# Batch 0's last kv from two terms, a later output copy, and two loads exchanged, in a fused attention and feed-forward kernel

## Chip, core, metric

One core of one Trainium2 chip. The time is that of one execution on the device in microseconds (us). Each kernel is run several times and checked against the reference; all runs told here were correct and none was more than 1.5% above the fastest run of its kernel. Profiles come from one further execution, and their times count from the start of the span.

## The reference, cut to what matters

```python
def phi(x): return where(x > 0, x, exp(x) - 1) + 1     # = max(x, 0) + min(exp(x), 1)
q_p, k_p = phi(q), phi(k)                              # (8 batches, 8 heads, 576, 64)
kv  = einsum('bhsd,bhse->bhde', k_p, v)
z   = sum(k_p, axis=2)
x   = (q_p . kv) / (q_p . z + 1e-6)                    # -> (4608 tokens, 512)
out = (silu(x @ w_gate) * (x @ w_val)) @ w_out         # d_ff = 1536
```

## The kernel before, cut

Tokens go through the feed-forward part in nine groups of 512. Almost all of the time is matmuls of 128x128 by 128x512. What is not hidden is the head: batch 0's attention has to be done before the first feed-forward matmul. The head pairs of a batch are `lp` 0 and 1; "x" is a normalised attention output, the operand of the first layer.

```python
r_copy(0, 0, 1, "VV")             # kv of pair 0 -> R (VectorE)
add_k(0, 1)                       # phi(k) of pair 1: min(exp k,1) + max(k,0)
t_corners(0, R, 0, X)             # numerators of pair 0
x_t(0, 0, X)                      # two x of pair 0 (VectorE)
kv_corner(0, 1, kp, True, True)   # kv of pair 1: 36 matmuls of 64x64
r_copy(0, 1, 2, "VV")
warm(WARM[7], ps=pp4[2][1])       # one matmul that only fills
l1_mm(0, 0, pp4[2], (0,))         # first feed-forward matmuls (L276)
l1_mm(0, 1, X, (0,))
t_corners(0, R, 1, pp4[1])
x_t(0, 1, pp4[1])
... (l1_mm for chunks 1, 2, 3; then the other blocks, L292)
```

Weights and the next batches' k, q and v are loaded by GpSimd on one queue (q0 of the page). They land in the order in which it issues them: of the loads below, those issued at 22.25, 23.57, 24.97 and 26.65 us in the kernel before land at 34.1, 35.5, 38.0 and 39.4. Group 0's second layer (L299) is interleaved with batch 1's attention: transposes of phi(q) (L370), then its x, then group 1's first matmuls.

```python
ld_w2(0, 4); ld(q, qr, 1, 0); ld_w2(4, 8); ld(q, qr, 1, 1); ld_w2(8, 12)
...
for t in range(4):
    if t == 3: nx(0, dz); nx(1, cq)             # numerators and x of batch 1
    for fb in range(FO, FB): l2_mm(0, t, fb)
    if t < 3: l2_out(0, t, "V")                 # output copy on VectorE
exp_k(2, 0); exp_k(2, 1)
l2_out(0, 3, "V")
```

## Time and profile before

| | before |
|---|---|
| time, median of 3 runs | 314.3 us (314.2 to 314.55) |
| span of the profile | 312.5 us |
| TensorE busy | 306.2 us, 98% |
| first feed-forward matmul (L276) starts | 14.34 us |
| batch 1's transposes (L370) start | 40.77 us |
| group 1's first matmul (L276) starts | 49.84 us |

In the profile PE is TensorE's matmuls, PEld its weight loads, DVE VectorE, ACT ScalarE, POOL GpSimd. A line of a timeline is: start, time, engine, line of the source, operation, out<-in, shapes, count, and in brackets the idle time before it and what ended it. Matmuls overlap: one of 512 columns shows 0.38 us, but in this trace the next starts 0.215 to 0.216 us after it. Below, a wait of TensorE is the distance of two starts less 0.2155.

### The profile page before, as it was taken

How to read it: one execution, taken by the hardware profiler on the slowest of the kernel's cores; microseconds unless marked ns; L12 is line 12 of the kernel's file. 1: busy time of each engine (PE TensorE's matmuls, PEld its weight loads, DVE VectorE, ACT ScalarE, POOL GpSimd, SP SyncE). 2: the span in 40 equal slices, each digit the busy share in tenths (PEclk: the TensorE clock that was granted, in tenths of full speed). 3: DMA queues.
4: the chain of work that ended last, by engine and by line, in shares of the span. 5: the costliest groups of instructions: out<-in, count | busy, mean ns of one | idle time of the engine just before them, and what ended most of it. 6: DMA issues, size and time to landing. Idle time of an engine off the chain costs nothing.

```text
span 312.5 us, 5494 instructions
## 1 busy us (share of the span) xinstructions
PE 306.2 (98%) x2169; PEld 142.3 (46%) x2169; DVE 204.0 (65%) x361; ACT 153.9 (49%) x232; POOL 47.4 (15%) x72
## 2 busy tenths in 40 slices
PE   8999999999999999999999999999999999999994
PEld 3444454444544454445444544454444444444442
DVE  4854859899699657976697759874981434143410
ACT  4955869639733845375535643475330333133311
POOL 8655334310000410032000500000000000000000
PEclk9999999999999999999999999999999999999999
DMA  8999999997512594139612990324032300140014
GB/s 218 198 196 200 207 206 240 231 206 127 116 26 41 92 192 117 38 50 183 171 37 39 131 235 3 73 45 92 2 69 57 86 1 1 39 97 0 0 36 101
DMA packets 41162, 32.80 MB, mean 105 GB/s; under 512 B 16432, under 2 KB 36144, under 8 KB 41136
## 3 DMA queue, kind: packets, MB, share of 16 engines
q0 software_dynamic: 20464, 18.29, 37.4%
q1 hardware_dynamic: 20592, 14.13, 18.8%
q8 instruction: 17, 0.28, 0.4%
q14 instruction: 9, 0.07, 0.1%
q10 hardware_dynamic: 80, 0.03, 0.0%
HBM read 37.75 MB, written 9.44 MB: 151 GB/s over the span
## 4 chain that ended last, share of the span: by engine, by line
PE 95%; DMA 1%; DVE 1%; ACT 1%; issue 0%; SPq 0%; DVEq 0%
PE pp L292 57%; PE pp L299 30%; PE pp L276 2%; PE pp L254 2%; PE pp L185 2%; DMA q<-in_q_dram 1%; PE pp L124 0%; ACT ek L120 0%; PE pp L398 0%; PE pp L370 0%; PE pp L429 0%; DVE xT L411 0%; ACT qT L120 0%; DVE kp L159 0%; PE pp L212 0%
## 5 line engine op out<-in xcount | busy, mean ns | idle before, releaser
L120 ACT ACTIVATE sil<-pp 128x512 f16<-128x512 f32 x108 | 63.4, 597 | 101.8 <-PE pp L292 100.0
L292 PE MATMUL pp<-xT,wg 128*128 128x512 f16 x416 | 106.8, 379 | 0.0
L292 PE MATMUL pp<-xT,wv 128*128 128x512 f16 x416 | 106.8, 379 | 0.0
L285 DVE SCALAR_TENSOR_TENSOR hT<-pp,sil 128x512 f16<-128x512 f32 x108 | 72.4, 681 | 48.8 <-PE pp L292 35.5
L299 PE MATMUL pp<-wo,hT 128*128 128x512 f16 (+2 forms) x444 | 97.1, 373 | 0.6 <-DVE osb L322 0.6
L299 PEld LDWEIGHTS <-hT 128*128 128x128 f16 x444 | 42.0, 98 | 49.8 <-issue 2.1
L292 PEld LDWEIGHTS <-wv 128*128 128x128 f16 x416 | 40.7, 98 | 49.1
L292 PEld LDWEIGHTS <-wg 128*128 128x128 f16 x416 | 40.7, 98 | 48.4
L322 DVE TENSOR_SCALAR osb<-pp 128x512 f32<-128x512 f32 (+1 forms) x19 | 12.9, 682 | 30.9 <-PE pp L299 26.5
L120 ACT ACTIVATE osb<-pp 128x512 f32<-128x512 f32 (+1 forms) x18 | 10.3, 574 | 34.8 <-PE pp L299 34.8
L120 ACT ACTIVATE ek<-kr 128x1152 f16<-128x1152 f16 x16 | 17.9, 1157 | 0.1
L120 ACT ACT_TABLE_LOAD x13 | 16.7, 1283 | 2.3 <-PE pp L292 2.1
L229 DVE TENSOR_TENSOR qp<-qp,rden 128x1152 f16<-128x1152 f16 x12 | 16.2, 1347 | 0.0
L220 DVE TENSOR_REDUCE den<-prod 128x18 f32<-128x1152 f16 x12 | 16.1, 1343 | 0.0
L120 ACT ACTIVATE eq<-qr 128x1152 f16<-128x1152 f16 (+1 forms) x15 | 16.0, 1102 | 0.1
L695 POOL COPY gate<-qT 128x1 f16<-128x1 f16 x4 | 1.0, 256 | 97.2 <-DMA qT<-qp 97.2
L271 DVE TENSOR_SCALAR xT<-pp 128x512 f16<-128x512 f32 (+1 forms) x14 | 8.8, 667 | 7.1 <-PE pp L254 7.1
L103 POOL DMA_DIRECT2D vr<-in_v_dram x16 | 11.7, 731 | 8.5 <-PE pp L292 2.6
L103 POOL DMA_DIRECT2D kr<-in_k_dram x16 | 11.5, 723 | 8.9 <-DMA vr<-in_v_dram 2.8
L159 DVE TENSOR_TENSOR kp<-ek,kp 128x1152 f16<-128x1152 f16 x16 | 12.1, 758 | 0.5
L103 POOL DMA_DIRECT2D qr<-in_q_dram x14 | 10.3, 736 | 6.7 <-DMA wo<-in_moe_w_out_dram 1.7
L147 DVE TENSOR_SCALAR ek<-ek 128x1152 f16<-128x1152 f16 x16 | 7.5, 470 | 5.7 <-ACT ek L120 5.5
(82 smaller groups left out, 179.5 us busy)
## 6 DMA issues: line engine op xcount, KB each, us to landing
out_dram<-osb SPq DMA_DIRECT2D x70, 128.0 KB, 3.4
kr<-in_k_dram POOLq DMA_DIRECT2D x16, 288.0 KB, 8.6
vr<-in_v_dram POOLq DMA_DIRECT2D x16, 288.0 KB, 9.9
qr<-in_q_dram POOLq DMA_DIRECT2D x14, 288.0 KB, 11.9
wo<-in_moe_w_out_dram POOLq DMA_DIRECT2D x3, 512.0 KB, 13.0
wg<-in_moe_w_gate_dram POOLq DMA_DIRECT2D x5, 256.0 KB, 8.7
wv<-in_moe_w_val_dram POOLq DMA_DIRECT2D x5, 256.0 KB, 9.3
q<-in_q_dram SPq DMA_DIRECT2D x2, 576.0 KB, 4.1
```

Of the source, the lines that this page charges most:

```text
L103: nc.gpsimd.dma_start(out=dst[b % NB][:, 2 * lp:2 * lp + 2, :], in_=src[b].rearrange("(l a) (c j) d -> (a c) l (j d)", a=2, j=J)[:, 2 * lp ...
L120: nc.scalar.activation(out=out, in_=in_, func=func, bias=bias, scale=scale)
L147: nc.vector.tensor_scalar(out=a, in0=a, scalar1=1.0, scalar2=None, op0=ALU.min)
L159: nc.vector.tensor_tensor(out=a, in0=ek[b % 2][:, lp, :, :], in1=a, op=ALU.add)
L185: nc.tensor.matmul(out=ps[hh][D * l2:D * l2 + D, D * lp:D * lp + D], lhsT=t[b % 2][rows, lp, j, D * l2:D * l2 + D], rhs=vr[b % NB][rows, 2 ...
L220: nc.vector.tensor_reduce(out=den[:, c, :], in_=prod[:, :, :].rearrange("p j (l d) -> p (j l) d", d=D), axis=AX.X, op=ALU.add)
L229: nc.vector.tensor_tensor(out=qv, in0=qv, in1=rden[:, c, :].unsqueeze(2).to_broadcast([P, 2 * J, D]), op=ALU.mult)
L271: nc.vector.tensor_scalar(out=dst, in0=ps[l2][:, c0:], scalar1=1.0 / SC, scalar2=None, op0=ALU.mult)
L285: nc.vector.scalar_tensor_tensor(out=hT[g % 2][:, fb, :], in0=ps[1][:, :], scalar=SC, in1=s[:, :], op0=ALU.mult, op1=ALU.mult)
L292: nc.tensor.matmul(out=ps[h][:, :], lhsT=w[:, c, P * fb:P * fb + P], rhs=xT[g % 2][:, c, :], start=(c == 0), stop=(c == 3))
L299: nc.tensor.matmul(out=l2p[(g, t)][:, n0:n1], lhsT=hT[g % 2][:, fb, P * t:P * t + P], rhs=wo[:, fb, n0:n1], start=(fb == 0), stop=(fb == F ...
L322: nc.vector.tensor_scalar(out=o[:, n0:n1], in0=ps[:, n0:n1], scalar1=1.0 / SC, scalar2=None, op0=ALU.mult)
```

## The change

The intent is to take waits out of the head and one from ahead of group 1. VectorE no longer makes phi(k) of pair 1; TensorE sums kv over both terms of it instead. The copies of R go between the first two x. Group 0's third output copy makes way for batch 1's x. And w_out's second third is loaded ahead of q, so that it is there in time for a second layer that starts earlier.

```diff
-    WARM = (4, 1, 4, 3, 2, 1, 1, 1)
+    WARM = (4, 1, 4, 3, 2, 1, 1)
@@ loads
     ld_w2(0, 4)
+    ld_w2(4, 8)
     ld(q, qr, 1, 0)
-    ld_w2(4, 8)
     ld(q, qr, 1, 1)
@@ head
-    add_k(0, 1)
     t_corners(0, R, 0, X)
-    x_t(0, 0, X)
-    kv_corner(0, 1, kp, True, True)
+    x_t(0, 0, X, (0,))
+    kv_corner(0, 1, kp, True, False)
+    kv_corner(0, 1, ek, False, True)
     r_copy(0, 1, 2, "VV")
-    warm(WARM[7], ps=pp4[2][1])
+    x_t(0, 0, X, (1,))
     l1_mm(0, 0, pp4[2], (0,))
+    t_corners(0, R, 1, pp4[1])
     l1_mm(0, 1, X, (0,))
-    t_corners(0, R, 1, pp4[1])
@@ group 0's second layer
-            if t < 3:
+            if t < 2:
                 l2_out(0, t, "V")
         exp_k(2, 0)
         exp_k(2, 1)
+        l2_out(0, 2, "V")
         l2_out(0, 3, "V")
```

## The prediction

What no trace or run of this case shows is cut out of the recorded text, and with it one of its four rivals. No term of its sum is among the cuts: it still comes to -0.10 + 0.18 - 0.20 = -0.12 us.

> **What bounds the kernel now.** I read the page first (busy shares), then the chain of work that ended last, then TensorE's waits, then the timelines of VectorE, TensorE and GpSimd around the three places that the change touches, and last the landings of single transfers. All times are microseconds from the start of the span.
>
> From the page:
>
> ```profile
> PE 306.2 (98%) x2169; PEld 142.3 (46%) x2169; DVE 204.0 (65%) x361; ACT 153.9 (49%) x232; POOL 47.4 (15%) x72
> ```
>
> TensorE is busy 98% of 312.5 us, and the chain puts 95% of the span on it. So a change can move the end only where TensorE waits, or where its own work grows or shrinks. After 52 us it hardly waits: a feed-forward stage in the chain is 96 matmuls in 20.72 us, 215.8 ns each. The listed waits are all at the head, except one of 0.6 us at the very end, which the change leaves alone. What the change can win is therefore in the first 50 us. The chain there:
>
> ```profile
> 12.98 0.68 DVE kp L159
> ...
> 13.70 0.48 PE pp L185 x36
> 14.18 0.32 PE pp L124
> 14.50 0.86 PE pp L276 x4
> ...
> 49.11 0.69 DVE xT L411
> ```
>
> The reader is to see that the chain crosses VectorE at 12.98 (the add that makes phi(k) for the second head pair) and at 49.11 (the first x of group 1). Between them it goes through the filler matmul L124 into the first L276 matmuls. The change attacks both crossings. VectorE's timeline at the first:
>
> ```profile
> 12.90 0.75 DVE L159 TENSOR_TENSOR kp<-ek,kp 128x1152 f16<-128x1152 f16 x1
> 13.56 1.28 DVE L411 SCALAR_TENSOR_TENSOR xT<-pp,rd 128x512 f16<-128x512 f32 x2
> 14.76 0.35 DVE L201 CAST R<-pp 128x64 f16<-128x64 f32 x2
> 15.81 1.29 DVE L411 SCALAR_TENSOR_TENSOR xT<-pp,rd 128x512 f16<-128x512 f32 x2 [0.70 <-PE pp L254]
> ```
>
> The kv result (R) was ready at 14.2, but its copies stand behind two x and start at 14.76. At the second crossing, in VectorE's and TensorE's timeline:
>
> ```profile
> 48.50 0.69 DVE L322 TENSOR_SCALAR osb<-pp 128x512 f32<-128x512 f32 x1 [0.18 <-PE pp L299]
> ...
> 49.11 2.47 DVE L411 SCALAR_TENSOR_TENSOR xT<-pp,rd 128x512 f16<-128x512 f32 x4
> ...
> 49.84 0.38 PE L276 MATMUL pp<-xT,wg 128*128 128x512 f16 x1
> ```
>
> The third output copy of group 0 stands directly ahead of the x that TensorE waits for. TensorE's last matmul before it starts at 49.41 (three from 48.96, about 0.22 apart), so it could go on at 49.62 and goes on at 49.84: 0.22 lost.
>
> The third place is in between. TensorE transposes batch 1's phi(q), which VectorE makes from a q that has to land:
>
> ```profile
> 37.63 0.29 DVE L392 TENSOR_TENSOR qp<-eq,qr 128x256 f16<-128x256 f16 x1
> 37.84 0.45 DVE L374 TENSOR_SCALAR qp<-qr 128x1152 f16<-128x1152 f16 x1
> 38.29 0.46 DVE L147 TENSOR_SCALAR ek<-ek 128x1152 f16<-128x1152 f16 x1
> ...
> 39.95 0.76 DVE L377 TENSOR_TENSOR qp<-qp,eq 128x1152 f16<-128x1152 f16 x1
> ```
>
> ```profile
> 40.77 0.62 PE L370 MATMUL pp<-id,qp 128*128 128x128 f16 x8
> ```
>
> The add ends at 40.71, the transposes start at 40.77. TensorE's last matmul before started at 40.51 and would have let it go on at 40.72. VectorE is just in time; nothing here is spare. GpSimd's timeline of issues and, for the two issues, the landings:
>
> ```profile
> 23.57 0.70 POOL L103 DMA_DIRECT2D qr<-in_q_dram  x1 [0.56 <-DMA wv<-in_moe_w_val_dram]
> 24.97 0.76 POOL L116 DMA_DIRECT2D wo<-in_moe_w_out_dram  x1 [0.71 <-DMA kr<-in_k_dram]
> ```
>
> ```profile
> qr<-in_q_dram POOLq DMA_DIRECT2D x1, 288.0 KB, 11.9
> ```
>
> ```profile
> wo<-in_moe_w_out_dram POOLq DMA_DIRECT2D x1, 512.0 KB, 13.0
> ```
>
> The last number is microseconds from issue to landing: q lands at 23.57 + 11.9 = 35.5, w_out's second third at 24.97 + 13.0 = 38.0. The same view gives the first third at 34.1 and q's second half at 39.4.
>
> [...]
> - [...] The page's PEclk row is 9 in all slices[...].
> - [...] from the L276 matmul at 14.98 to the 64x64 corners at 15.29 are 0.31 us, not 0.22; about 0.09 per switch.
> - [...] The landings above come in the order of issue, so exchanging two issues exchanges who lands first.
> - [...] 0.70 us spans, 11.9 us landings. So I use landings only.
>
> **The change part by part.**
>
> *Head.* It removes one VectorE add (0.75) and one filler matmul (0.22 of issue), and adds 36 small kv matmuls (64x64), because kv is now summed over max(k,0) and min(exp k,1) instead of over their sum. The two R copies (0.35) move between the two x.
>
> 1. First x of group 0. It needs the corners of R. The first starts at 12.90, but the second of the same bank waits for the second R copy, starts about 13.04 and ends, at 0.40 each, at 13.44. In the later case the corners end at 15.70 and x starts at 15.81, so x follows by 0.11: 13.55. It starts at 13.56 today. Taking the add away thus gains nothing on the first x.
> 2. kv of the second head pair no longer waits for the add. It can start behind the corners at about 13.26; 72 small matmuls take 0.73 (chain at 46.98: L185 x72, 0.73). It ends about 14.0 to 14.1 where today it ends at 14.18. The doubled work hides in the time before the first x is done.
> 3. R copies: behind the first x, at 14.16 instead of 14.76. Second x about 14.41 to 15.09.
> 4. TensorE: from the start of an x to the matmul that reads it are 0.73 (49.11 to 49.84), so the first L276 is at 13.55 + 0.73 = 14.29; today 14.34, behind the filler. Then two matmuls, corners of R (ready at about 14.6) after 0.52, the next matmul 0.34 later, 14 at 0.2155: L292 at 14.29 + 3.88 = 18.17, today 18.28. Today's 0.05 wait for the third x falls away too. Head gain: about 0.10.
>
> *Loads.* q lands behind w_out's second third. Bytes are the same, so it lands when that third lands today, about 38.0 (34.1 + 2.5 + 1.4). VectorE wants q at 37.84 less the 0.10, so 37.74, and now starts at about 38.0. The next operation, min on exp k, no longer waits for ScalarE and follows after 0.37 instead of 0.45; then 0.50, 0.68, 0.49 and 0.76 as today, and 0.05 to TensorE: transposes at about 40.85. Today 40.77; with the head gain TensorE would be there at 40.62. So the head gain is eaten and about 0.08 more lost. What the exchange wins is nothing: w_out's second third lands at 38.0, and its first matmul is at 35.54 + 16 x 0.2155 = 38.99, so it was a microsecond early already. Behind this point VectorE has 0.7 to spare at the second set of transposes (add ends 42.24, transposes 42.95), so 0.08 does not grow.
>
> *Output copy.* Without the 0.69 copy ahead, x of group 1 needs only its corners. The first four pairs end at 48.81; VectorE's sequencer sees that by 48.85, and an x follows such a mark by 0.065 in the head: 48.91 instead of 49.11. TensorE goes on at 48.91 + 0.73 = 49.65 instead of 49.84, gain 0.20, of a possible 0.22. The second x moves with it. The copy now costs VectorE 0.6 before batch 2's phi(k), less the 0.2 gained. Its next products (hT) wait for the table load and the SiLU that end about 56.0, and phi(k) ends 55.34 today, so 0.4 fits.
>
> Sum: -0.10 at the head, +0.18 at the transposes, -0.20 at x: **-0.12 us**, so 314.3 becomes 314.2 us.
>
> **The rivals.**
> - *Nothing is eaten at the transposes.* If q lands nearer 37.7, the head gain stays: -0.30, 314.0. For it: GpSimd issues are paced by earlier landings and could slip either way. Against: the queue moves the same bytes, and w_out transfers took 2.5 to 2.6 and q 1.4 between landings.
> - *q lands later or ScalarE becomes the wait.* ScalarE's exp of q starts at 38.16 today and needs the same q; if q lands at 38.2, everything to the transposes slides 0.2 more: about 314.4.
> - *The doubled kv is on the path.* If 72 small matmuls took as long as 2 x 0.48 = 0.96, R is done at 14.25, copies at 14.3, the corners can go at 14.75, and TensorE asks for them at 14.81: still hidden. Only beyond that does it cost.
> - [...]
>
> **Range and chances.** The three runs of before spread over 0.35 us, and the terms above can each be off by 0.1 to 0.2. So 313.85 to 314.5 should hold it 8 times in 10. Two per cent would be 6.3 us; all waits of TensorE before 50 us that the change touches are below 0.7 us. Chance of within 2%: 0.985; faster 0.005, slower 0.01.
>
> **What would show it.** In the changed kernel's timeline: first x at 13.55 and first L276 at 14.29; L292 from about 18.17; q's landing at 38.0 and VectorE's max on q (L374 today) starting at that moment, with a wait on DMA named; transposes at 40.85 with TensorE idle about 0.2 before; group 1's first x without a copy ahead, TensorE's L276 about 0.12 earlier than 49.84. The prediction is wrong if q lands in time (the gain is then 0.3), if R's copies wait for kv beyond 14.4, if VectorE falls behind after 52 us and TensorE shows waits there, or if PEclk shows a slice below 9.

## The result

The changed kernel took 314.83 us (median of 4; 314.69 to 314.99), the kernel before 314.28 (median of 4; 314.2 to 314.55). The ratio is 1.0016, 95% interval 0.9999 to 1.0033. Here and below a ratio is the mean time of one kernel's runs over that of the other's in the same rounds, so it is not quite the ratio of the medians. By the medians the change costs about half a microsecond where 0.1 was to be won, and 314.83 lies above the range; the interval just holds no effect at all, and a second set of runs (after_again, below) gives 1.0012 (1.0 to 1.0024). What follows therefore rests on the traces more than on the times.

The page of the changed kernel says only that TensorE did slightly more:

```profile
PE 306.5 (98%) x2204; PEld 143.0 (46%) x2204; DVE 203.3 (65%) x360; ACT 153.9 (49%) x232; POOL 47.3 (15%) x72
```

The head works on VectorE as intended (its timeline; the first x, the two R copies, then the rest):

```profile
13.53 0.69 DVE L411 SCALAR_TENSOR_TENSOR xT<-pp,rd 128x512 f16<-128x512 f32 x1 [0.57 <-ACT rd L120]
14.14 0.35 DVE L201 CAST R<-pp 128x64 f16<-128x64 f32 x2
...
15.31 1.36 DVE L411 SCALAR_TENSOR_TENSOR xT<-pp,rd 128x512 f16<-128x512 f32 x2 [0.23 <-ACT lnt L120]
```

Then TensorE, in the list of who waited for whom, has a wait that the kernel before does not have, and no releaser is named for it ("issue"):

```profile
PE pp L276 <- issue: 0.8, 1, 0.8
```

TensorE's timeline shows where:

```profile
16.66 0.38 PE L276 MATMUL pp<-xT,wv 128*128 128x512 f16 x1
16.87 0.38 PE L276 MATMUL pp<-xT,wg 128*128 128x512 f16 x1
18.02 0.38 PE L276 MATMUL pp<-xT,wv 128*128 128x512 f16 x1 [0.76 <-issue]
18.23 0.38 PE L276 MATMUL pp<-xT,wg 128*128 128x512 f16 x1
```

The matmul at 18.02 comes 1.14 us after the one before, 0.93 more than 0.2155. The load that brought its weights, its x and its accumulator had all served matmuls ahead of it, its own weight load had started at 16.88, and the trace shows no semaphore that it waits for. It is row 448 of TensorE's program (branch, weight loads and matmuls counted from 0). So TensorE did not wait for data; it seems not to have had the instruction.

The second crossing went as foreseen (timeline at batch 1's x):

```profile
49.72 1.29 DVE L411 SCALAR_TENSOR_TENSOR xT<-pp,rd 128x512 f16<-128x512 f32 x2 [0.59 <-PE pp L254]
...
50.47 0.38 PE L276 MATMUL pp<-xT,wg 128*128 128x512 f16 x1
```

No output copy stands ahead of x any more; VectorE waits 0.59 us for the numerators instead. TensorE's wait ahead of group 1 fell from 0.22 to 0.04.

The stages of all profiles, worked out from the starts in TensorE's timeline (us): A is the start of the first L276, B from there to the first L292, C to the first transpose, D to group 1's first matmul, E to the first L292 after that group's second layer (83.54 in the kernel before), F to the end.

| profile | A | B | C | D | E | F |
|---|---|---|---|---|---|---|
| before | 14.34 | 3.94 | 22.49 | 9.08 | 33.69 | 228.98 |
| changed | 14.27 | 4.82 | 22.49 | 8.89 | 33.81 | 228.94 |
| changed, again | 14.47 | 4.35 | 22.66 | 8.89 | 33.79 | 229.01 |
| head_only | 14.45 | 4.62 | 22.68 | 9.07 | 33.82 | 228.95 |
| rows_only | 14.85 | 4.47 | 22.49 | 9.08 | 33.85 | 229.01 |
| plus8 | 14.91 | 5.28 | 22.49 | 8.89 | 33.81 | 229.03 |
| minus8 | 14.17 | 3.90 | 22.79 | 8.89 | 33.82 | 229.03 |
| minus32 | 14.40 | 3.90 | 22.69 | 8.89 | 33.83 | 229.02 |
| copy_only | 14.60 | 3.94 | 22.49 | 8.89 | 33.79 | 229.01 |
| swap_only | 14.21 | 3.94 | 22.80 | 9.08 | 33.69 | 229.02 |
| best | 14.17 | 3.90 | 22.68 | 8.89 | 33.82 | 229.01 |

A moves by some 0.7 us from profile to profile, whatever the kernel; the landing of the first k accounts for part of it (7.95 us in the kernel before, 8.56 in plus8, but 7.28 in copy_only, whose A is 14.60). The other columns repeat within 0.1 us where nothing was changed, apart from two effects in C and E that are told below, so small effects are read from them and not from A or the total. From before to changed: -0.07 in A, +0.88 in B, 0.00 in C, -0.19 in D, +0.12 in E, -0.04 in F, in all +0.70; the spans are 312.5 and 313.2.

**Theories.** F, instruction fetch: TensorE's program arrives in blocks, and the 70 rows that the change adds bring TensorE to the end of what it has before the next block is there. What the traces show that could be such blocks is 17 packets of 16,384 bytes of kind "instruction" on queue 8, in both kernels. That they are TensorE's is the author's reading. For it, only TensorE's program is of that order: 4340 rows in the kernel before, 255 to a packet, where VectorE has 361 instructions on the page and the others fewer. And from the start of the 14th packet to that of the 17th, TensorE starts 768 rows in the kernel before and 766 in the changed one, 256 to a packet. (The changed kernel, with 4410 rows, has 17 packets too, so the count is no exact match. Row 448 is no multiple of 256 either; the runs do not show what precedes it in the blocks.) The first starts at 15.54 us in the changed kernel. The DMA view of the stretch from 15.5 to 15.6 (queue, packets, MB, share of 16 engines; a packet counts whole where it starts, so a share can pass 100%) has it:

```profile
q0 software_dynamic: 39, 0.02, 146.1%
q8 instruction: 1, 0.02, 60.9%
```

The trace gives it 0.97 us, and TensorE goes on 2.48 us after its start. In the kernel before it starts at 15.30, and TensorE is at about row 364 then; it reaches row 448 at 24.75 us, long after. Rival T: the tighter order of the head, or the sum over two terms, makes the stall. Rival W: the exchange of the loads makes it.

### The profile page after: what moved, and what is told of

Its sections match the earlier page's. It is cut to its first block, busy times and chain, and to the rows that moved or that the text cites. A ratio compares the mean times of both kernels' runs of the same rounds, so it can differ in the third digit from the quotient of the medians.

```text
span 313.2 us, 5562 instructions
## 1 busy us (share of the span) xinstructions
PE 306.5 (98%) x2204; PEld 143.0 (46%) x2204; DVE 203.3 (65%) x360; ACT 153.9 (49%) x232; POOL 47.3 (15%) x72
## 4 chain that ended last, share of the span: by engine, by line
PE 95%; ACT 1%; DMA 1%; DVE 1%; issue 1%
PE pp L292 57%; PE pp L299 30%; PE pp L276 2%; PE pp L254 2%; PE pp L185 2%; DMA q<-in_q_dram 1%; PE pp L429 1%; ACT lnt L120 0%; ACT ek L120 0%; PE pp L370 0%; PE pp L124 0%; DVE xT L411 0%; ACT qT L120 0%; ACT rd L120 0%; PE pp L212 0%
## 5 line engine op out<-in xcount | busy, mean ns | idle before, releaser
L292 PE MATMUL pp<-xT,wg 128*128 128x512 f16 x416 | 106.7, 379 | 0.0
L292 PE MATMUL pp<-xT,wv 128*128 128x512 f16 x416 | 106.7, 379 | 0.0
L292 PEld LDWEIGHTS <-wv 128*128 128x128 f16 x416 | 40.7, 98 | 49.1
L292 PEld LDWEIGHTS <-wg 128*128 128x128 f16 x416 | 40.7, 98 | 48.5
L159 DVE TENSOR_TENSOR kp<-ek,kp 128x1152 f16<-128x1152 f16 x15 | 11.4, 758 | 0.5
```

The source lines that it names most:

```text
L159: nc.vector.tensor_tensor(out=a, in0=ek[b % 2][:, lp, :, :], in1=a, op=ALU.add)
L292: nc.tensor.matmul(out=ps[h][:, :], lhsT=w[:, c, P * fb:P * fb + P], rhs=xT[g % 2][:, c, :], start=(c == 0), stop=(c == 3))
```

## The experiments

All outputs are right.

**rows_only.** The kernel before, with meaningless small matmuls where TensorE waits for the add anyway (0.26 us in the trace of the kernel before):

```diff
     x_t(0, 0, X)
+    dummy(35)      # 35 matmuls of 64x64 on a constant, into an accumulator written again later
     kv_corner(0, 1, kp, True, True)
```

> The kernel before, with 35 meaningless 64x64 matmuls (70 rows of TensorE's program, no change of order elsewhere) placed in the time in which TensorE waits for the add. Theory F (instruction fetch): in the changed kernel TensorE stood still for 0.93 us at row 448 of its program, with no wait named[...]; only the number of rows ahead matters. Then the same row stalls here, until about 18.0 us, for about 0.8 us, and the kernel takes about 315.1 us. Rival T (the tighter order itself, or kv from two terms, makes the stall): no stall, 314.3 us.

Measured: 315.05 us against 314.3, ratio 1.0018 (1.0002 to 1.0033). TensorE's timeline:

```profile
17.50 0.38 PE L276 MATMUL pp<-xT,wg 128*128 128x512 f16 x1
18.24 0.38 PE L276 MATMUL pp<-xT,wv 128*128 128x512 f16 x1 [0.36 <-issue]
```

The matmul at 18.24 is again row 448, here in the old order, with the old sum. The stall is 0.53 and not 0.8 us: row 448 was due at 17.72, which is 0.63 later than in the changed kernel (17.09), mostly by A, while TensorE went on only 0.23 later, with a packet that started 0.40 later (15.94). T falls, and with it W: neither the order, nor the sum, nor the loads were changed here.

**plus8, minus8, minus32.** The changed kernel with 8 rows more, 8 fewer and 32 fewer ahead of the place. Fewer rows come from doing a part of the add after all, in time in which VectorE is idle (0.57 us ahead of the first x in the changed kernel):

```diff
 # plus8
+    dummy(4)
     kv_corner(0, 1, kp, True, False)
 # minus8: n = 1;  minus32: n = 4
+    a = kp[0][:, 1, J - n:J, :]
+    nc.vector.tensor_tensor(out=a, in0=ek[0][:, 1, J - n:J, :], in1=a, op=ALU.add)
     t_corners(0, R, 0, X)
     ...
-    kv_corner(0, 1, ek, False, True)
+    kv_corner(0, 1, ek, False, True, J - n)    # only the j that were not added
```

> The changed kernel with 4 small meaningless matmuls (8 rows) more ahead of the stalled place. F with a block that arrives at a fixed time: row 448 is reached four matmuls earlier, the stall grows from 0.93 to about 1.8 us but ends at the same time near 18.0 us, and the time grows by about 0.86 us to about 315.7 us. F with a fetch asked for at a row: stall stays near 0.9 us and the time at 314.8 us. T: 314.8 us, stall at the same matmul.

> The changed kernel, with the add done for one of the nine j and 8 rows fewer ahead of the stalled place. F with a block that arrives at a fixed time (about 18.0 us): row 448 comes four matmuls (0.86 us) later, so the stall falls from 0.93 to about 0.07 us and the time from 314.83 to about 314.0 us. F with a fetch asked for at a row near the stalled one: the stall stays near 0.9 us. T: the stall stays at the same matmul, 314.8 us.

> The changed kernel, with the add done for four of the nine j in VectorE's idle time and 32 rows fewer. F: row 448 comes 3.4 us later than the block, no stall; then the steps of the prediction can be seen without it: L292 from about 18.17 us, transposes held by q's landing near 38 us, total about 314.1 to 314.2 us. T: stall stays, 314.8 us.

Measured: plus8 315.72 us, ratio 1.0039 (1.0023 to 1.0054); minus8 314.63, ratio 1.0007 (0.999 to 1.0023); minus32 314.54, ratio 1.0001 (0.9987 to 1.0015); before 314.3 in the same rounds. TensorE's timeline of plus8 and of minus8 at row 448:

```profile
16.64 0.38 PE L276 MATMUL pp<-xT,wg 128*128 128x512 f16 x1
18.25 0.38 PE L276 MATMUL pp<-xT,wv 128*128 128x512 f16 x1 [1.22 <-issue]
```

```profile
17.64 0.38 PE L276 MATMUL pp<-xT,wg 128*128 128x512 f16 x1
17.85 0.38 PE L276 MATMUL pp<-xT,wv 128*128 128x512 f16 x1
```

The place moves with the row, by four matmuls for 8 rows, and the stall with it: 1.39 us in plus8, none in minus8 and minus32. Counted from the first L276, plus8 is due at row 448 after 1.95 us and the changed kernel after 2.82, which is the 0.86 of four matmuls. In every profile that stalls, TensorE goes on 2.3 to 2.5 us after the packet's start: 15.54 and 18.02, 15.94 and 18.24, 15.89 and 18.25. In minus8 the packet starts at 15.23 and row 448 is due at 17.85, 2.6 us later: just enough. F in its first form holds: the block comes at its own time, not at a row near the stall, and TensorE waits for it if it is early. (The totals of minus8 and minus32 are 0.3 to 0.6 us above what was expected, and by time alone minus8 cannot be told from the kernel before; it is the traces that show the stall gone.)

Without the stall, minus8 and minus32 show the steps of the prediction. B is 3.90 against 3.94 before. C is longer by 0.30 and 0.20, since q holds the transposes. In minus32 (q's landing, VectorE's max on q, the transposes, each from its view):

```profile
qr<-in_q_dram POOLq DMA_DIRECT2D x1, 288.0 KB, 13.0
```

```profile
38.14 0.46 DVE L374 TENSOR_SCALAR qp<-qr 128x1152 f16<-128x1152 f16 x1
```

```profile
40.98 0.28 PE L370 MATMUL pp<-id,qp 128*128 128x128 f16 x2
```

q was issued at 25.1 and landed 13.0 later, at 38.1; the max starts at once, and TensorE's wait ahead of the transposes is 0.24 us, where the prediction's 40.85 against 40.62 makes 0.23. (In minus8, minus32 and swap_only an operation of VectorE ahead of this max had also been held up, as told under best; without q the max could have started only 0.10 to 0.15 earlier.)

**head_only.** The kernel before with the change's head; loads and output copy as before.

> The kernel before with the change's head alone. F: the stall at row 448 is here whole (0.93 us, until about 18.0 us), the order of w_out and q and the output copy have no part in it: 314.28 + 0.82 = 315.1 us. If the w_out/q order made the stall or the lost DMA time: no stall and 314.2 us.

Measured: 315.3 us against 314.32, ratio 1.0032 (1.0008 to 1.0056). Its list of waits has the line again:

```profile
PE pp L276 <- issue: 0.6, 1, 0.6
```

It stalls 0.73 us at row 448 (packet 15.54, on again at 17.99). The exchange of the loads and the moved copy have no part in it. C is longer by 0.19 here too, although q lands at 35.7; I come back to this.

**copy_only.** The kernel before with the third output copy moved.

> The kernel before with group 0's third output copy behind batch 1's x, alone. The step of the prediction: x of group 1 begins 0.20 us earlier, TensorE's wait of 0.22 us before it falls to about 0.03 us, 314.1 us. Rival (the copy delays batch 2's phi(k), and TensorE waits later): gain gone, 314.3 us.

Measured: 314.4 us against 314.32, ratio 0.9998 (0.9984 to 1.0012). Its timeline:

```profile
49.17 1.29 DVE L411 SCALAR_TENSOR_TENSOR xT<-pp,rd 128x512 f16<-128x512 f32 x2 [0.59 <-PE pp L254]
...
49.92 0.38 PE L276 MATMUL pp<-xT,wg 128*128 128x512 f16 x1
```

D falls from 9.08 to 8.89, as predicted. But E grows by 0.10. The loss lies in the burst of 96 small matmuls of batch 2 and 3's attention near 80 us, as a pause of 0.1 us between two of them. The total, 314.4, misses the 314.1 that was expected. All other profiles of the table have the pause too, even rows_only and head_only, where the copy is in its old place, so the moved copy, which the expectation's rival meant, is not needed for it. The kernel before and swap_only have it not. Nor do TensorE's rows decide it: copy_only has TensorE's program of before, and gate4 (below), with that of the changed kernel, has E at 33.69. What it is I have not found out.

**swap_only.** The kernel before with the two loads exchanged.

> The kernel before with w_out's second third ahead of q, alone. The step of the prediction: q lands near 38.0 us instead of 35.5, VectorE's max on q starts there with a wait, the transposes start near 40.85 instead of 40.77 us: 314.35 to 314.4 us. Rival (q lands in time): 314.3 us and no wait.

Measured: 314.52 us against 314.32, ratio 1.0007 (0.9991 to 1.0022). VectorE's timeline and TensorE's:

```profile
38.11 0.46 DVE L374 TENSOR_SCALAR qp<-qr 128x1152 f16<-128x1152 f16 x1
```

```profile
40.95 0.34 PE L370 MATMUL pp<-id,qp 128*128 128x128 f16 x3 [0.19 <-DVE qp L377]
```

q lands at 38.08 and the max starts at 38.11. TensorE waits 0.36 us ahead of the transposes where it waited 0.05 before, and C is 0.31 longer. The step is right in kind and too small in size: without the head's gain it was put at 0.08. In this profile q was 0.1 later than worked out and the head 0.13 earlier than in the profile of before (A), which makes 0.31. (The medians differ by 0.2, and the interval of the ratio holds no effect at all.) Nothing is won for it: no wait for w_out is in either profile.

**best.** minus32's head, the moved copy, the loads in the order of before.

> Head with the add for four of nine j (32 rows fewer), copy moved, loads in the order of before. F: no stall; head gain 0.10, the 0.045 us wait at the transposes as before, copy gain 0.20: 314.28 - 0.30 = 314.0 us. If the stall has another cause: 314.6 us or more.

Measured: 314.24 us against 314.32, ratio 0.9995 (0.9981 to 1.001): no stall, but not to be told from the kernel before, and 0.24 above what was expected. C is 0.19 longer, though q was there at 35.6. In its timeline, GpSimd's issue of a load and a VectorE operation of 0.70 us, which takes 0.45 in the profile before:

```profile
35.84 0.71 POOL L103 DMA_DIRECT2D qr<-in_q_dram  x1 [0.69 <-DMA qr<-in_q_dram]
...
36.10 0.70 DVE L143 TENSOR_SCALAR kp<-kr 128x1152 f16<-128x1152 f16 x1
```

The operation starts while GpSimd issues, and ends 0.25 after it. The same is found in head_only (0.65 instead of 0.45, beside an issue that ends 0.26 earlier) and in swap_only (0.46 instead of 0.22). Being under way together is not enough. In the profile before the same operation starts 0.19 into the issue and keeps its 0.45, and the issue takes 0.79 instead of 0.71:

```profile
35.78 0.79 POOL L103 DMA_DIRECT2D qr<-in_q_dram  x1 [0.70 <-DMA qr<-in_q_dram]
35.97 0.45 DVE L143 TENSOR_SCALAR kp<-kr 128x1152 f16<-128x1152 f16 x1
```

Over all 13 profiles, the 53 TENSOR_SCALAR operations of this shape that start 0.27 to 0.45 into an issue are all held until 0.25 to 0.29 after its end, and none of the 85 that start earlier than 0.25 into one is held. No run took the issues away, so the issue as the reason is argued from these counts, not shown. What a hold costs can be read where nothing else in VectorE's order changed: in head_only this one ends ahead of the transposes,

```profile
40.25 0.65 DVE L155 TENSOR_SCALAR eq<-eq 128x1152 f16<-128x1152 f16 x1
```

and C is 0.19 longer; in after_again one of 0.64 instead of 0.45 makes C 0.17 longer; in copy_only one of 0.58 falls ahead of an idle time of VectorE and costs nothing. In best an operation ahead of the held one had already started 0.34 late for a reason that I have not found, so its 0.19 is not the hold's alone.

**gate4, gate3, after_again.** Why is the block late? The changed kernel, but GpSimd issues a load (the seventh to the sixteenth) only when the load d before it has landed, d = 4 or 3. It copies one column of that load's destination to a scrap tile first, and so waits:

```diff
+        if 6 <= n < 16:
+            nc.gpsimd.tensor_copy(out=gate[:, :], in_=ahead[n - d])
```

and the changed kernel itself once more beside them.

> The changed kernel; from the seventh load to the sixteenth GpSimd issues a load only when the load four before it has landed, so fewer bytes wait in the queue when TensorE's block of instructions is asked for. Theory Q (the block's transfer waits behind the loads issued before it): its packet starts about 1 us earlier than 15.5 us, the stall at row 448 is gone or under 0.2 us, and the time is about 314.0 to 314.3 us if the weights still arrive in time. Theory N (its start has nothing to do with the loads): packet at 15.2 to 15.9 us and a stall of 0.5 to 0.9 us as before, 314.8 us.

> The same with three instead of four loads under way. Q: the packet starts near 13.7 us, about 1.6 us earlier than in the changed kernel, no stall at row 448. N: packet at 15.2 to 15.9 us and the stall as in the changed kernel. If the queue runs empty, loads land later and TensorE waits for weights by name, which is neither.

> The changed kernel once more, on the chip of the two gated ones. F: a wait of TensorE at row 448 with no releaser named, until about 2.4 us after the instruction packet's start, 0.5 to 0.95 us long, as in the first profile; 314.8 us. If it was a chance of the first profile: no such wait.

Measured: gate4 318.52 us, ratio 1.0126 (1.0102 to 1.015); gate3 321.73, ratio 1.0227 (1.0212 to 1.0243); after_again 314.93, ratio 1.0012 (1.0 to 1.0024); before 314.45 in the same rounds. gate4's DMA view from 12.4 to 12.5, and its TensorE timeline at row 448 (L286 is L276 here):

```profile
q8 instruction: 1, 0.02, 102.9%
```

```profile
16.88 0.38 PE L286 MATMUL pp<-xT,wg 128*128 128x512 f16 x1
17.09 0.38 PE L286 MATMUL pp<-xT,wv 128*128 128x512 f16 x1
```

The packet starts at 12.42 us, in gate3 at 12.59, 3 us earlier than in the changed kernel (I had expected 1 and 1.6), and with all the rows of the changed kernel ahead of it, row 448 does not stall. So the block's transfer waits for the loads that GpSimd has issued: Q. In which queue or engine it waits, the runs do not show. One load fewer under way (gate3) does not bring it further forward.

How late the block is can be estimated from the end of the kernel, where GpSimd's loads are done (the last lands at 187 us in the changed kernel). There, in all 13 profiles, the 14th and the 17th packet start when TensorE has started 144 to 150 rows more than a multiple of 256. If the first is asked for at the same place, that is at 10.8 to 10.9 us in these kernels (row 146), and it starts 4.8 us after it in the changed kernel and 1.7 us after it in gate4 and gate3. That it is asked for there in the head too is not shown.

after_again stalls as the first profile did, but for half as long: 0.45 us at the same row (on again at 17.74, packet at 15.44). As kernels the gated ones are bad: the queue runs thin, and from the third pair on the feed-forward weights land 1.3 to 2.8 us later in gate4 than in the changed kernel. TensorE then waits for weights by name (0.7 us at the longest) and for the phi(q) that VectorE makes late (1.9 us).

## Why the prediction was wrong

- **Head, steps 1 and 3 right.** First x 13.53 (predicted 13.55), R copies 14.14 (14.16), first L276 14.27 (14.29). That they fit to 0.02 us is in part luck: in the second profile of the same kernel they all come 0.2 later (A is 14.47). And step 1 has the right time with half the reason. It names the corners of R alone; the profile names ScalarE's rd (the reciprocal denominators), ready at 13.47, 0.05 after the corners at 13.42. In minus32 the corners are the last.
- **Head, steps 2 and 4: the step that failed.** Step 2 priced the 36 added matmuls by their time ("The doubled work hides in the time before the first x is done"), which is right, and not by the 70 rows that they and the removed filler leave in TensorE's program. Step 4 then let 14 matmuls follow "at 0.2155" to L292 at 18.17. They did so up to row 447, at 16.88; then TensorE stood 0.93 us, by theory F without an instruction, and L292 came at 19.09. Without the stall (minus8, minus32, best) stage B is 3.90, 0.04 below before, as step 4 has it. None of the four rivals named instruction fetch; the list of what would prove it wrong did not hold it either.
- **Loads: right in kind, hidden in the result.** The wait for q is real (0.24 in minus32 where 0.23 was worked out; 0.36 in swap_only). In the first profile of the changed kernel it does not show, because the stall had made TensorE later than q: C is unchanged. In the second, with half the stall, C is 0.17 longer, but not by q, which had landed 0.18 before its max: that is the held operation told under best.
- **Output copy: right.** Predicted gain 0.20, measured 0.19 in D in all kernels that have it.
- **"After 52 us it hardly waits": not quite.** 0.10 to 0.16 us more is spent in E in every profile of the table but swap_only's. Its cause stays open.
- **Sum.** Predicted -0.12. With the stall (+0.93), without the loads' 0.18 and with the 0.12 near 80 us it is +0.75; the spans differ by 0.70, the medians by 0.55.

## What to carry to other kernels

Here an instruction cost its place in the program as well as its time: 70 rows more brought a stall of 0.45 to 0.93 us at row 448 in four profiles, 78 more one of 1.39, and 62 more none. Before many small matmuls are added to a short head, look when the instruction packets start and count the rows that TensorE has started by then (here about 364 at 15.30 us in the kernel before and 435 at 15.54 in the changed one, which stalled at row 448). In five profiles a wait of TensorE for which the profile names no releaser, at a matmul whose operands are all in use already, marked that stall. In the kernel before and in the changed one, with seven and eight loads issued and not landed, the packet started at 15.30 and 15.54 us; in gate4 and gate3, which from the seventh load to the sixteenth let at most four and three be under way, at 12.42 and 12.59. Fewer rows ahead of row 448 helped (no stall in minus8 and minus32), and holding back the loads cost more than it saved here (318.5 and 321.7 us).
